# All 160 attention steps of the second branch moved into the segment loop of the first

## The chip, the cores and the metric

The kernel runs on one core of a Trainium2 chip. The metric is the device time of one execution in microseconds (us). A kernel is run several times in each round, beside the kernel before on the same chip, and the median of its runs is quoted. The profile page names the engines PE (matmul), PEld (its weight loads), DVE (VectorE), ACT (ScalarE), POOL (GpSimd) and SP (SyncE, which issues nearly all DMAs here).

## The reference, cut to what matters

Two attention branches over the same 2048 positions are mixed by a gate. Branch A goes through 64 segments of 32 rows one after the other, because the 8 memory rows of a segment come out of the one before it. Branch B attends causally inside four chunks of 512 rows, with 32 heads of 16 columns, and adds a linear-attention memory that the earlier chunks leave.

```python
# A: serial over 64 segments, 32 heads of 128
for s in range(n_seg):
    h = concatenate([mem, x[s*32:(s+1)*32]])        # 8 + 32 rows
    q, k, v = h @ Wq, h @ Wk, h @ Wv
    o = softmax(mask(q k^T * scale)) v
    o = o @ Wo
    mem = o[:8];  outs.append(o[8:])
# B: four chunks of 512 rows, 32 heads of 16
for s in range(4):
    a_dot = softmax(qs ks^T * scale + mask) vs
    a_mem = phi(qs) M / (phi(qs) z + 1e-6)
    o = g * a_mem + (1 - g) * a_dot
    M = M + phi(ks)^T vs;  z = z + sum(phi(ks))
# mix
out = gate * a + (1 - gate) * (b @ wo)
```

## The kernel before

The kernel is a Python program that emits instructions in a fixed order for each engine. Branch A's segment is a list of units (`A_ORDER`). Since A is a serial chain, work that does not depend on it is put between its units: the projections of the next segments' "left" rows (`Fc`, `Ff`), and the steps of B (`bS` scores, `bP` times V, `bT` the chain that divides and adds the memory term).

B's attention is cut into 16 jobs (four chunks, four groups of 8 heads) of ten steps each, 160 steps in all. A job first needs its keys and queries (`KTj`, `QTj`), then its values and memory (`Vj`, `pQj`, `MZj`), which the projections had stored in DRAM.

```python
def load(self, job, part):                       # class BAttn
    ...
    if part == "k":
        for e in range(2):
            for t in range(4):                   # eight DMAs of 16 KB
                o = 32 * t + 16 * e
                ld(v.KTj[par][e][o:o + 16, :], v.kTd[sb, f, o:o + 16, :], ...)
        ld(v.QTj[par][:, :], v.qTd[sb, f], ...)  # a ninth of 128 KB
        return
    ld(v.Vj[par][:, :, :], v.vd[sb, :, :, 136 * f:136 * (f + 1)], ...)
    if sb > 0:
        ld(v.pQj[par][:, :], ...);  ld(v.MZj[par][:, :], ...)

def scores(self):
    n = self.n; self.n += 1
    job, G, k = n // 10, (n // 5) % 2, n % 5     # G: which 4 of the 8 heads
    ...
    r = slice(64 * G + 32 * x, 64 * G + 32 * x + 32)    # partitions read
    ins = pe.matmul(..., KT[e][r, 128 * kc:128 * (kc + 1)], QT[r, q0:q0 + w], ...)
    ...
    if n % 10 == 9:                              # last step of the job:
        self.load_next(job, "k")                 # the next job's K and Q
```

`par` picks one of two buffers for the first 40 steps. These run ahead of the segment loop, between the pieces of the projections. For the other 120 steps, which run in segments 0 to 50, there is one buffer. The order of a segment, and the pace of the steps:

```python
n_pre = DEV.get("n_pre", 40)
for n in range(n_pre):                           # ahead of the segments
    bat.scores()
    while pieces and done < 10 + n * rate:
        piece()                                  # a projection
    ...
    if n > 1:
        bat.pv()
...
A_ORDER = """
    K1 K0 Q0 Q1 Fc TK0 TQ0 TK1 Ff bP TQ1 bT Fc S0 bS V0 M0 S1 N0 V1 M1 N1 PV0 Fc E0a E0b PV1 W0 E1a E1b W1 Fc bP bP bS
    WT bS Ff bT""".split()
...
nseg_b = DEV.get("nseg_b", 51)
target = min(bat.total, n_b0 + -(-(bat.total - n_b0) * (s + 1) // (nseg_b)))
def b_s():
    if bat.n < target and bat.n - bat.pv_n < 2:
        bat.scores()
```

`S`, `M`, `N`, `PV`, `E`, `W` and `WT` are A's own scores, sums, normalization, product with V, evacuation, output product and transposition into the next segment's memory rows. `N1` makes the tile `Pn_sb` that `PV1` reads.

## Time and profile before

The median is 1159.68 us; the profiled run's span is 1153.9 us. The first lines of the profile page of the kernel before: span, busy time of each engine, and three rows of the 40 slices (tenths of busy time, granted PE clock, DMA).

```profile
span 1153.9 us, 54295 instructions
...
PE 1012.0 (88%) x24359; PEld 559.7 (49%) x24389; DVE 491.1 (43%) x1229; ACT 692.1 (60%) x1427; POOL 248.7 (22%) x573
...
PE   4667769999999999999999999999999998988886
...
PEclk8798779999999999999999999999999998999999
DMA  9486310010101001010100001010100000000000
```

PE is at 4 to 7 tenths in the first six slices, and at 9 from there nearly to the end. So there are two stages. The table by stretches of the kernel before has the columns PE, PEld, DVE, ACT and POOL busy us with instruction counts, then granted clock, DMA share and GB/s. I cut it at the first pass of A (164 us), the first copy of memory rows into `hT` (188), the copy 56 segments later (1045) and the last copy (1132).

```profile
0.00:164.00 164.00, 104.20 (x871) 53.65 (x885) 54.57 (x106) 67.68 (x91) 85.46 (x176) 0.82 0.59 197
164.00:188.00 24.00, 22.25 (x462) 11.25 (x464) 8.34 (x18) 11.92 (x25) 1.60 (x5) 0.91 0.01 3
188.00:1045.00 857.00, 797.70 (x20687) 446.62 (x20696) 386.92 (x1006) 557.74 (x1181) 155.08 (x375) 1.00 0.06 17
1045.00:1132.00 87.00, 73.97 (x1993) 40.76 (x1992) 34.66 (x86) 46.38 (x112) 6.14 (x17) 1.00 0.04 9
1132.00:1154.00 22.00, 13.84 (x351) 7.42 (x352) 6.62 (x16) 8.39 (x20) 0.40 (x1) 0.94 0.03 8
```

In the first row PE is busy for 104.20 of 164 us, at a clock of 0.82: this is the stage that the change attacks. In the third row it is busy for 797.70 of 857 us at full clock: this stage is bound by PE.

Two places matter. The first is a job change, where the last step of one job is followed by the first step of the next, which needs new K and Q. In the timeline of the kernel before (start, duration, engine, line, operation, out<-in, count), the eight K loads are issued from 231.23 on, the Q load at 235.70, and the next score step comes at 238.79. Q had landed at 237.83, so nothing waited.

```profile
230.69 0.39 PE L726 MATMUL ps<-QTa,KTa 32*128 32x256 bf16 x4
231.23 4.43 SPq L685 DMA_DIRECT2D KTa<-scr_kTd  x8
...
235.70 0.42 SPq L685 DMA_DIRECT2D QTa<-scr_qTd  x1
```

The second is the gap between the two products with V (L1102), of which the second needs the normalized `Pn_sb`. Here a half left pass (L876, 0.62 us) stands between them, and 0.36 us of idle time are left.

```profile
516.32 0.27 PE L1102 MATMUL ps<-Pn_sb,V_sb 32*128 32x40 bf16 x16
...
516.64 0.62 PE L876 MATMUL ps<-Wv_sb,xL 128*32 128x512 bf16 x8
517.62 0.28 PE L1102 MATMUL ps<-Pn_sb,V_sb 32*128 32x40 bf16 x16 [0.36 <-DVE Pn_sb L1092]
517.92 2.18 PE L1139 MATMUL ps<-Wo_sb,OT_sb 128*32 128x512 bf16 x32
```

The view of waits of the kernel before sums them up (us in total, times, longest). Of the 13.1 us for Q, 11.8 are one wait ahead of the segments; in the middle of the segments they are 1.3.

```profile
PE ps L1102 <- DVE Pn_sb L1092: 25.4, 62, 0.9
...
PE ps L726 <- DMA QTa<-scr_qTd: 13.1, 5, 11.8
```

### The profile page before, as it was taken

What the parts mean: (1) busy time and instruction counts of PE and PEld (TensorE: products, weight loads), DVE (VectorE), ACT (ScalarE), POOL (GpSimd) and SP (SyncE); (2) the same over time, 40 slices, a digit from 0 to 9 for tenths busy, and PEclk for the clock granted to TensorE, in tenths of its full rate; (3) what the DMA queues carried; (4) which work ended last, traced back from release to release, by engine and by line L of the source; (5) the groups of instructions that cost most, each with busy time, mean ns of one, the idle gap of its engine ahead of it and who ended that gap; (6) DMA issues with size and microseconds to landing.
All of it is one profiled execution on the core that took longest, in us unless ns stands there. A gap on an engine that the chain in (4) does not pass through costs nothing. (4 is left out here: it accounts for less than half of the span.)

```text
span 1153.9 us, 54295 instructions
## 1 busy us (share of the span) xinstructions
PE 1012.0 (88%) x24359; PEld 559.7 (49%) x24389; DVE 491.1 (43%) x1229; ACT 692.1 (60%) x1427; POOL 248.7 (22%) x573
## 2 busy tenths in 40 slices
PE   4667769999999999999999999999999998988886
PEld 2333325555555555555555555555555554544443
DVE  2333334444444444444444444444444443434333
ACT  2455336666666666666666666666666664555554
POOL 6554431211212121212122111212122110000000
PEclk8798779999999999999999999999999998999999
DMA  9486310010101001010100001010100000000000
GB/s 309 141 278 226 105 62 3 3 32 4 36 5 27 13 11 29 8 32 8 27 12 23 12 9 31 8 33 7 28 12 23 18 3 21 3 12 4 12 12 7
DMA packets 50943, 47.59 MB, mean 41 GB/s; under 512 B 23184, under 2 KB 49176, under 8 KB 49176
## 3 DMA queue, kind: packets, MB, share of 16 engines
q1 hardware_dynamic: 50712, 44.13, 12.3%
q8 instruction: 192, 3.15, 1.1%
q14 instruction: 39, 0.32, 0.1%
HBM read 31.50 MB, written 12.61 MB: 38 GB/s over the span
## 5 line engine op out<-in xcount | busy, mean ns | idle before, releaser
L742 POOL TENSOR_SCALAR_AFFINE_SELECT PTa<-PTa 128x256 bf16<-128x256 bf16 (+1 forms) x205 | 90.1, 440 | 419.1 <-ACT PTa L734 387.6
L734 ACT ACTIVATE PTa<-ps 128x1024 bf16<-128x1024 f32 x147 | 150.4, 1024 | 42.2 <-PE ps L726 40.6
L876 PE MATMUL ps<-Wv_sb,hT 128*32 128x512 bf16 x2048 | 134.9, 381 | 2.0 <-ACT QT_sb L312 1.3
L312 ACT ACTIVATE QN_sb<-ps 128x512 bf16<-128x512 f32 x128 | 76.4, 597 | 89.5 <-PE ps L876 89.5
L876 PE MATMUL ps<-Wk_sb,hT 128*32 128x512 bf16 x2048 | 123.3, 383 | 3.7 <-DVE hT L1166 2.6
L1139 PE MATMUL ps<-Wo_sb,OT_sb 128*32 128x512 bf16 x2048 | 126.2, 381 | 0.1
L876 PE MATMUL ps<-Wq_sb,hT 128*32 128x512 bf16 x2048 | 121.6, 379 | 0.0
L314 DVE CAST V_sb<-ps 128x512 bf16<-128x512 f32 x128 | 88.5, 691 | 73.1 <-PE ps L1077 40.5
L1149 DVE TENSOR_TENSOR aW_sb<-ps,aW_sb 128x256 bf16<-128x256 f32 x128 | 48.4, 420 | 128.1 <-ACT aW_sb L312 126.1
L312 ACT ACTIVATE aW_sb<-ps 128x256 bf16<-128x256 f32 x128 | 42.2, 381 | 92.5 <-PE ps L1139 92.5
L1191 POOL COPY OTL<-OT_sb 128x256 bf16<-128x256 bf16 x64 | 25.4, 397 | 319.4 <-DVE OT_sb L314 319.4
L312 ACT ACTIVATE OT_sb<-ps 128x320 bf16<-128x320 f32 x192 | 75.7, 428 | 24.9 <-PE ps L1111 24.9
L312 ACT ACTIVATE QT_sb<-ps 128x512 bf16<-128x512 bf16 x128 | 77.0, 601 | 22.3 <-PE ps L885 22.3
L876 PEld LDWEIGHTS ps<-Wq_sb,hT 128*32 128x32 bf16 x2048 | 54.8, 97 | 55.8
L726 PE MATMUL ps<-QTa,KTa 32*128 32x512 bf16 (+1 forms) x448 | 55.6, 305 | 24.4 <-DMA QTa<-scr_qTd 13.1
L314 DVE CAST KN_sb<-ps 128x512 bf16<-128x512 f32 x64 | 44.2, 690 | 75.6 <-PE ps L876 75.6
L876 PEld LDWEIGHTS ps<-Wk_sb,hT 128*32 128x32 bf16 x2048 | 49.2, 97 | 53.5 <-DVE hT L1166 5.1
L314 DVE COPY KT_sb<-ps 128x512 bf16<-128x512 bf16 x64 | 27.2, 425 | 111.0 <-PE ps L885 111.0
L1139 PEld LDWEIGHTS ps<-Wo_sb,OT_sb 128*32 128x32 bf16 x2048 | 46.6, 95 | 49.9 <-ACT OT_sb L312 20.7
L876 PEld LDWEIGHTS ps<-Wv_sb,hT 128*32 128x32 bf16 x2048 | 47.2, 95 | 38.1 <-issue 6.7
L312 ACT ACTIVATE KN_sb<-ps 128x512 bf16<-128x512 f32 x64 | 38.2, 597 | 43.2 <-PE ps L876 43.0
L1081 ACT ACTIVATE R_sb<-ps 128x160 f32<-128x160 f32 x128 | 38.8, 303 | 33.7 <-PE ps L1077 33.3
(146 smaller groups left out, 1802.5 us busy)
## 6 DMA issues: line engine op xcount, KB each, us to landing
Wk_sb<-in_A_Wk_dram SPq DMA_DIRECT2D x4, 1024.0 KB, 7.9
Wq_sb<-in_A_Wq_dram SPq DMA_DIRECT2D x4, 1024.0 KB, 5.6
Wv_sb<-in_A_Wv_dram SPq DMA_DIRECT2D x4, 1024.0 KB, 6.4
Wo_sb<-in_A_Wo_dram SPq DMA_DIRECT2D x4, 1024.0 KB, 6.3
scr_vd<-V SPq DMA_DIRECT2D x16, 136.0 KB, 2.2
Wo_sb<-in_A_x_dram SPq DMA_DIRECT2D x4, 512.0 KB, 8.2
scr_kTd<-stgk SPq DMA_DIRECT2D x16, 128.0 KB, 3.9
scr_qTd<-stgq SPq DMA_DIRECT2D x16, 128.0 KB, 4.6
```

What stands on the lines that cost most here:

```text
L312: P.op("act", lambda a: a.activation(dst, src, ACT.Copy), reads=[v.rbank[k] for k in bks], writes=dres, name=name)
L314: P.op("dve", lambda d: d.tensor_copy(dst, src), reads=[v.rbank[k] for k in bks], writes=dres, name=name)
L726: ins = pe.matmul(v.pb[bks[x]][:, o:o + w], KT[e][r, 128 * kc:128 * (kc + 1)], QT[r, q0:q0 + w], start=True, stop=True, tile_position=(r.s ...
L734: P.op("act", lambda a: a.activation(pt[:, :, :], v.ps[:, bks[0]:bks[1] + 1, :], ACT.Exp, scale=v.SCALE_B), reads=[v.rbank[b] for b in bks ...
L742: P.op("gp", lambda g, mv=mv: g.affine_select(mv, mv, [[0, mv.shape[1]], [1, 128]], ALU.is_ge, 0.0, base=0, channel_multiplier=-1), reads= ...
L876: ins = pe.matmul(pb[bk][SEG * j:SEG * (j + 1), :], lhs(c), w_sb[:, c, n0:n0 + 512], start=(c == 0), stop=(c == C - 1))
L1081: P.op("act", lambda a: a.activation(R_sb[:, b, :], pb[bk][:, 224:384], ACT.Ln), reads=[rbank[bk]], writes=[Rs("R%d" % b)], name="ln%d_%d" ...
L1139: ins = pe.matmul(pb[bk][SEG * j:SEG * (j + 1), :], OT_sb[:, h, 0:SEG], Wo_sb[:, h, :], start=(b == 0 and i == 0), stop=(b == 1 and i == 3))
L1149: P.op("dve", lambda d, cs=cs: d.tensor_tensor(aW_sb[:, 1, cs], pb[bk][:, cs], aW_sb[:, 0, cs], ALU.subtract), reads=[rbank[bk], Rs("aWh%d ...
L1191: P.op("gp", lambda gq: gq.tensor_copy(OTL[par][:, :, 8 * r:8 * r + 8], OT_sb[:, :, SEG:L]), reads=[Rs("OT%d_%d" % (c, hf)) for c in range ...
```

## The change

The intent: B's first 40 steps stretch the stage before the segments, where PE is badly used. With all 160 steps in the segments, that stage holds projections alone. B then lags behind A, so A's finished rows are parked in DRAM until the B chunk of the same rows is through. The second set of job buffers goes, staging gets deeper, the pieces of the projections come in another order, part of their work moves from POOL to DVE, the engine assignment changes, and the left passes are no longer cut in halves. The diff, cut to its core:

```diff
-    n_pre = DEV.get("n_pre", 40)
-    bat = v.bat = BAttn(v, n_pre)
...
+    bat = v.bat = BAttn(v)
+    for n in range(len(pieces)):                      # projections only
...
+        pieces[n]()
...
     for part in "kv":
-        for job in range(2):
-            bat.load(job, part)
-    for n in range(n_pre):
-        bat.scores()
...
+        bat.load(0, part)
... (BAttn: one buffer throughout)
         if n % 10 == 9:
-            self.load_next(job, "k")
+            self.load(job + 1, "k")
... (pv: the chain of the job before is forced if its V load is not out yet)
+        while self.late and (job, "v") not in self.loaded:
+            self.run_late(1)
         self.load(job, "v")
...
 A_ORDER = """
-    K1 K0 Q0 Q1 Fc TK0 TQ0 TK1 Ff bP TQ1 bT Fc S0 bS V0 M0 S1 N0 V1 M1 N1 PV0 Fc E0a E0b PV1 W0 E1a E1b W1 Fc bP bP bS
-    WT bS Ff bT""".split()
+    bS K0 Q0 K1 Q1 TK0 TQ0 TK1 V0 bP TQ1 bP bT S0 Fc M0 S1 N0 V1 M1 PV0 E0a N1 E0b Ff PV1 W0 E1a E1b bS W1 Fc bS bP WT
+    Ff bT Ff""".split()
-A_ENG = dict(K0="dve", K1="act", Q0="act", Q1="act", V0="dve", V1="dve", TK0="dve", TK1="act",
-             TQ0="act", TQ1="act", E0a="act", E0b="act", E1a="act", E1b="dve", last=1)
+A_ENG = dict(K0="dve", K1="act", Q0="dve", Q1="act", V0="act", V1="dve", TK0="act", TK1="dve",
+             TQ0="dve", TQ1="act", E0a="act", E0b="act", E1a="dve", E1b="act", last=1)
...
-    n_b0, nseg_b = bat.n, DEV.get("nseg_b", 51)
+    n_b0, nseg_b = bat.n, DEV.get("nseg_b", 57)
... (left_units: one pass of four 128-row blocks instead of two halves)
-                for part in range(2):
-                    def u(...):
-                        proj(bk, lhs, w_sb, b, 2 * part, 2 * part + 2, ...)
+                def u(...):
+                    proj(bk, lhs, w_sb, b, ...)
... (A's rows parked, and fetched with B's rows for the last product)
+            P.dma(..., lambda sp: sp.dma_start(v.aTd[g], aT_st[par][:, :, :]), ...)
...
+        P.dma(..., lambda sp: sp.dma_start(aTg[:, :, :], v.aTd[g]), ...)
```

## The prediction

> What bounds it now. The page gives PE 88% of 1153.9 us, but there are two stages. Until 164.3 us (timeline: first pass with Wk and xL) the projections run with 40 of the 160 attention steps of B; the table by stretches shows PE 45 to 77% busy there, clock mostly 0.80 to 0.89, DMA 0.3 to 0.9. The 64 segments then take 990 us. With B steps in them PE is 93 to 94% busy at clock 1.00: about 15.2 us from one memory-row copy (hT, DVE) to the next, 0.9 of it PE idle, mostly 0.36 before the second PV (waits for Pn) and 0.32 before the WT transposition (timeline). So PE and its order bound the segments; evacuation chains and DMA bound the prologue.
>
> Removed. 40 steps leave the prologue. What stays is 60 projections of four 512-column matmuls (0.87 us at full clock in the timeline), transposes, and DMA: 16.5 us of first inputs, ten 1 MB weights at about 3.4, some 60 stores at 0.34, together 71 us; PE, from 7 us on, needs about as long. POOL leaves the phi chain (1.48 us each), staging is deeper. First pass at about 82 us (75 to 95): -82 us.
>
> Added, steady. A step costs PE 0.32 (scores) + 0.29 (PV) us; 2.8 instead of 2.35 steps in a segment, over 57 segments. Usually nothing stands between the two PVs now, so the chain from the second half's sums to Wo (1.8 us) shows about 1.0 us idle instead of 0.4; the WT wait shrinks, because the Fc there is a whole 0.87 us pass. About 15.5 us a segment: +19. Without the stall at 965-986 us: -6. Waits for Wo at the start: +3. A second row group is left for after the last segment; its DMAs (1.7 to 2.8 us each) are serial: +8. Fewer fillers in the last segments: +3.
>
> Added, new waits. KTj/QTj have one buffer. The next job's nine loads start when its predecessor's tenth score step is done, and land 6.4 to 7.2 us after the first issue (timeline). Before, the following step came a long stretch later: PE waited for QTa only 1.3 us in all segments. Now two score slots stand 2 us apart at the segment's end and a third opens the next one. By the order of instructions, 9 of 15 job changes fall there: 4 with about 6 us of waiting, 4 with 5, 1 with 3.6: 48 us. In four segments both PVs of a job change are neighbours, so the V load (3.6 us) is waited for: 14 us. The Trainium skill ("TensorE: Matmul & The Clock Gate", Part 1) says that an idle window of about 3.4 us halves the PE clock; the trace agrees once in the segments (3.8 us idle, 0.5 for 6.8 us). Estimate: +10.
>
> Sum of spans: 1154 - 82 + 19 - 6 + 3 + 8 + 3 + 62 + 10 = 1171. I lean a little lower for overlaps: 1168 us; 1130 to 1200 should hold it 8 times in 10. Faster by over 2%: 0.2; within: 0.48; slower: 0.32.
>
> Right if: first left pass near 82 us; PE waits for QTj on DMA of 35 to 55 us in 9 segments, for Vj of 10 to 15; clock dips after them; undisturbed B segments of about 15.5 us.
>
> Wrong if: stores behind weights hold the prologue longer, or the clock stays halved after most waits (slower); the new engine assignment closes the gap before the second PV (faster).

## The result, and the profile after

The changed kernel took 1195.99 us (median of 4 runs, 1193.82 to 1199.4) against 1159.55 (1157.56 to 1160.88) for the kernel before in the same rounds. The ratio is 1.0318, with a 95% interval of 1.0289 to 1.0347: slower by 3.2%. A ratio here and below is the mean time of one kernel's runs over that of the other's of the same rounds, so it is not quite the ratio of the quoted medians. The forecast of 1168 us had the right sign and was 28 us short; the time lies inside the range of 1130 to 1200. A slowdown by over 2% had been given a chance of 0.32, less than the 0.48 for no clear change.

The profile page of the changed kernel, the same rows:

```profile
span 1192.1 us, 54216 instructions
...
PE 1026.2 (86%) x24389; PEld 553.3 (46%) x24389; DVE 513.3 (43%) x1309; ACT 671.2 (56%) x1371; POOL 212.5 (18%) x544
...
PE   8968997899789799979998999698978899999874
...
PEclk9989999899989899999999999899989999999997
```

The first slices are now at 8 and 9, as intended. But the 9s of the long stage have holes, and at several of them the clock row has an 8. The table by stretches of the changed kernel, cut at the same events:

```profile
0.00:82.00 82.00, 66.08 (x425) 33.57 (x429) 46.19 (x94) 34.56 (x59) 24.65 (x91) 0.96 0.86 282
82.00:111.00 29.00, 24.58 (x480) 11.67 (x480) 8.98 (x20) 12.46 (x25) 1.96 (x6) 0.89 0.73 236
111.00:1068.00 957.00, 840.62 (x21119) 457.51 (x21118) 411.40 (x1077) 572.46 (x1162) 177.93 (x427) 0.97 0.08 20
1068.00:1158.00 90.00, 77.20 (x2012) 41.76 (x2012) 38.91 (x100) 43.17 (x106) 7.55 (x20) 0.98 0.06 16
1158.00:1192.00 34.00, 17.75 (x364) 8.82 (x361) 7.81 (x18) 8.54 (x20) 0.40 (x1) 0.78 0.11 28
```

The first stage gave 82 us back (164 to 82). The same 56 segments went from 857 to 957 us: PE is busy for 43 us more, and idle for 57 us more (116 instead of 59). Where the idle time sits is told by the waits of the changed kernel:

```profile
PE ps L704 <- DMA QTj<-scr_qTd: 40.5, 9, 5.1
...
PE ps L1078 <- DVE Pn_sb L1068: 39.1, 43, 1.1
...
PE ps L751 <- DMA MZj<-scr_mzd: 10.6, 3, 3.7
...
PE ps L751 <- DMA Vj<-scr_vd: 2.6, 1, 2.6
```

Nine of the 15 job changes wait for the K and Q loads (L704 is the score step), and three and one for the memory and value loads (L751 is the step's product with V). The timeline of the changed kernel at one of the nine shows how. The tenth step of a job is at 745.81, and the next score step stands only two units later:

```profile
745.81 0.39 PE L704 MATMUL ps<-QTj,KTj 32*128 32x256 bf16 x4
...
746.23 3.56 SPq L664 DMA_DIRECT2D KTj<-scr_kTd  x8
...
746.80 0.25 PE L1136 MATMUL ps<-selL,aW_sb 128*128 128x32 bf16 x4 [0.16 <-DVE aW_sb L1125]
...
749.84 0.42 SPq L664 DMA_DIRECT2D QTj<-scr_qTd  x1
...
752.01 0.61 PE L704 MATMUL ps<-QTj,KTj 32*128 32x512 bf16 x2 [4.96 <-DMA QTj<-scr_qTd]
752.55 1.90 PE L855 MATMUL ps<-Wk_sb,hT 128*32 128x512 bf16 x16
754.23 1.92 PE L855 MATMUL ps<-Wq_sb,hT 128*32 128x512 bf16 x16
755.94 1.78 PE L855 MATMUL ps<-Wk_sb,hT 128*32 128x512 bf16 x16
757.55 1.03 PE L855 MATMUL ps<-Wq_sb,hT 128*32 128x512 bf16 x16
```

Two things are to be read here. First, the nine loads are issued one after the other, about 0.45 us apart, and the last had landed at 751.88, 5.65 us after the first issue. Each of the nine lands within 1.5 to 2.0 us of its own issue. (At the other job changes in the segments of this kernel the loads are 0.45 to 0.60 us apart, and the last lands 5.6 to 7.2 us after the first issue.) The Trainium skill ("DMA: Bandwidth & Descriptors", section "Anatomy of one DMA — SWDGE (gpsimd) path") gives a fixed cost of about 2.0 us for a DMA of another path, most of it completion. The trace agrees in size for these loads from SP, and shows what that single figure does not: the issues of a list add up. Second, after the wait the passes of 16 matmuls start 1.7 us apart (752.55, 754.23, 755.94, 757.55), where a pass takes 0.87 us elsewhere: PE ran at half clock, from 750.6 to 757.4, for 6.8 us. The same skill ("TensorE: Matmul & The Clock Gate", Part 1, "What's actually happening") says that the clock halves after an idle window of about 3.4 us, and that the window runs free of the program. The trace agrees in kind and not in the length: each of the 13 waits for job loads in the segments, 2.65 to 5.12 us long, has one stretch of 3.4 or 6.8 us at 0.5 that begins before the wait ends or up to 0.6 us after it, and three of these waits are shorter than 3.4 us (2.65, 2.84 and 3.32). The 13 stretches are 65 us together; the kernel before has one of 6.8 us in its segments. The length of the wait alone doesn't decide: a wait of 2.63 us in e5 was followed by no such stretch. Part of a stretch is still waiting time: here PE waited until 752.01. Of the 65 us, 15 lie inside the waits, and in the other 50 PE is busy throughout.

A whole segment of this kind beside its undisturbed neighbours, in the table by stretches of the changed kernel:

```profile
731.00:747.00 16.00, 14.92 (x386) 8.24 (x384) 6.47 (x16) 10.94 (x22) 3.10 (x8) 1.00 0.01 4
747.00:775.00 28.00, 18.30 (x378) 9.01 (x376) 8.02 (x23) 9.88 (x21) 3.23 (x7) 0.82 0.11 27
```

With nearly the same number of matmuls it took 28 us instead of 16: 9.7 us idle instead of 1.1, and 3.4 us more of busy time for the same work, at a clock of 0.82.

The other new loss is small but comes in most segments. With the left passes whole and `Fc` moved away, nothing stands between the two products with V. In the timeline of the changed kernel the wait for `Pn_sb` is 0.94 us instead of 0.36:

```profile
120.43 0.27 PE L1078 MATMUL ps<-Pn_sb,V_sb 32*128 32x40 bf16 x16
120.55 0.25 PE L1087 MATMUL ps<-Pn_sb,VL 32*128 32x16 bf16 x16
121.73 0.28 PE L1078 MATMUL ps<-Pn_sb,V_sb 32*128 32x40 bf16 x16 [0.94 <-DVE Pn_sb L1068]
```

The span by parts, with a segment measured from one copy of memory rows (`hT` on DVE) to the next:

| part | before | after | difference |
|---|---|---|---|
| to the first pass of A | 164.3 | 81.9 | -82.4 |
| to the first memory-row copy | 23.6 | 28.7 | +5.1 |
| next 56 segments | 856.8 | 957.6 | +100.8 |
| six segments without B | 87.1 | 89.9 | +2.7 |
| to the end | 22.0 | 33.9 | +11.9 |
| span | 1153.9 | 1192.1 | +38.2 |

In the 56 segments of the changed kernel, 43 have a mean of 15.73 us, and 13 (the ones with a job change that waits) are together 76.8 us longer than that. So the +100.8 are 76.8 of disturbance and 24.0 in everything else.

### The profile page after: what moved, and what is told of

It reads as the page before. It is cut to its first block, busy times and chain, and to the rows that moved or that the text cites. A ratio compares the mean times of both kernels' runs of the same rounds, so it can differ in the third digit from the quotient of the medians. Undisturbed runs are those within 1.5% of the kernel's fastest.

```text
span 1192.1 us, 54216 instructions
## 1 busy us (share of the span) xinstructions
PE 1026.2 (86%) x24389; PEld 553.3 (46%) x24389; DVE 513.3 (43%) x1309; ACT 671.2 (56%) x1371; POOL 212.5 (18%) x544
## 4 chain that ended last, share of the span: by engine, by line
PE 73%; ACT 9%; DVE 7%; DMA 5%; SPq 3%; issue 3%; POOL 1%; ACTq 0%; POOLq 0%; DVEq 0%
PE ps L855 35%; PE ps L1115 8%; PE ps L864 6%; PE ps L704 4%; SPq L664 3%; PE ps L751 3%; PE ps L583 2%; ACT PT L712 2%; PE ps L558 2%; DVE Pn_sb L1064 2%; PE ps L1078 2%; DMA QTj<-scr_qTd 2%; PE ps L918 2%; PE ps L964 1%; ACT R_sb L1057 1%
## 5 line engine op out<-in xcount | busy, mean ns | idle before, releaser
L712 ACT ACTIVATE PT<-ps 128x1024 bf16<-128x1024 f32 x160 | 163.3, 1022 | 99.1 <-PE ps L704 95.3
L855 PE MATMUL ps<-Wk_sb,hT 128*32 128x512 bf16 x2048 | 142.5, 401 | 0.7 <-DVE hT L1142 0.6
L720 POOL TENSOR_SCALAR_AFFINE_SELECT PT<-PT 128x256 bf16<-128x256 bf16 (+1 forms) x224 | 98.4, 439 | 223.8 <-ACT PT L712 215.3
L855 PE MATMUL ps<-Wq_sb,hT 128*32 128x512 bf16 x2048 | 137.1, 389 | 0.0
L1169 POOL COPY OTL<-OT_sb 128x256 bf16<-128x256 bf16 x64 | 25.4, 397 | 545.3 <-DVE OT_sb L321 432.9
L319 ACT ACTIVATE KN_sb<-ps 128x512 bf16<-128x512 f32 x64 | 38.2, 597 | 128.7 <-PE ps L855 128.7
L704 PE MATMUL ps<-QTj,KTj 32*128 32x384 bf16 (+3 forms) x512 | 64.8, 310 | 41.5 <-DMA QTj<-scr_qTd 40.5
L1078 PE MATMUL ps<-Pn_sb,V_sb 32*128 32x40 bf16 x2048 | 36.4, 178 | 44.5 <-DVE Pn_sb L1068 39.1
L751 PEld LDWEIGHTS ps<-Vj,PT 128*128 128x128 bf16 x1280 | 44.5, 96 | 55.7 <-issue 39.4
L751 PE MATMUL ps<-Vj,PT 128*128 128x17 bf16 x1280 | 57.4, 172 | 14.9 <-DMA MZj<-scr_mzd 10.6
L321 DVE COPY QT_sb<-ps 128x512 bf16<-128x512 bf16 x64 | 27.2, 425 | 99.5 <-PE ps L864 99.5
L1064 DVE TENSOR_TENSOR Pn_sb<-P_sb,R_sb 128x160 bf16<-128x160 bf16 x128 | 44.1, 345 | 51.0 <-ACT R_sb L1060 42.2
```

The costliest lines, as they stand in the source:

```text
L319: P.op("act", lambda a: a.activation(dst, src, ACT.Copy), reads=[v.rbank[k] for k in bks], writes=dres, name=name)
L321: P.op("dve", lambda d: d.tensor_copy(dst, src), reads=[v.rbank[k] for k in bks], writes=dres, name=name)
L704: ins = pe.matmul(v.pb[bks[x]][:, o:o + w], KT[e][r, 128 * kc:128 * (kc + 1)], QT[r, q0:q0 + w], start=True, stop=True, tile_position=(r.s ...
L712: P.op("act", lambda a: a.activation(pt[:, :, :], v.ps[:, bks[0]:bks[1] + 1, :], ACT.Exp, scale=v.SCALE_B), reads=[v.rbank[b] for b in bks ...
L720: P.op("gp", lambda g, mv=mv: g.affine_select(mv, mv, [[0, mv.shape[1]], [1, 128]], ALU.is_ge, 0.0, base=0, channel_multiplier=-1), reads= ...
L751: ins = pe.matmul(v.pb[ob][:, o:o + 17], pt[:, x, col:col + 128], V[:, kc, 17 * h:17 * (h + 1)], start=first, stop=True, skip_group_check= ...
```

## Experiments

The theory: the gain of 82 us is real, and it is more than eaten by the single-buffered loads at the job changes, including the half clock after them. The rivals: the order and engine assignment of the segment are simply worse; or the 40 steps cost more in the segments than they freed. The kernel before had medians of 1159.78 (e1 to e4), 1160.65 (e5 to e8) and 1159.09 us (e9 and e10). Each edit is made to the changed kernel. All ten are faster than the changed kernel, the slowest (e4) by 28 us.

### e1_nseg56: another phase of the job changes

Nothing is changed but the pace, and with it where in the segment each job changes. By the order of instructions, 8 of the 15 changes then fall where there is time, and no chain is forced.

```diff
-    n_b0, nseg_b = bat.n, DEV.get("nseg_b", 57)
+    n_b0, nseg_b = bat.n, DEV.get("nseg_b", 56)
```

> One number changed: the 160 steps of B are spread over 56 segments instead of 57. Theory A (waits for single-buffered K/Q and V loads at job changes make the loss): counted from the order of the slots, 9 bad K changes (8 of them under 2 us apart) and 4 neighbouring V changes become 7 K changes of about 3.5 us and no V change. PE waits for QTj fall from 40.5 to about 25 us, for Vj/MZj from 15 to about 0, and the clock stays at 1.00 nearly throughout: 1140 to 1158 us. Theory B (the 40 moved steps simply cost more PE time in the segments than they cost ahead of them): same work, 1190 to 1200 us. Theory C (the new order with an empty gap between the two PVs makes the loss): 1190 to 1200 us.

Measured: 1151.47 us (1148.0 to 1155.78), ratio 0.9932 (0.9896 to 0.9967), correct. One constant is worth 44.5 us, and brings the kernel under the kernel before. The waits for QTj fell from 40.5 us in nine to 19.7 in six; those for Vj went. Six job changes still wait 3.1 to 3.6 us for QTj, and their segments are 5 to 6 us longer than the others, more than the wait: all six have a stretch at half clock of 3.4 or 6.8 us. (A seventh waits 2.1 us for DVE and has none.) One of the six, in the timeline of e1:

```profile
206.93 0.61 PE L704 MATMUL ps<-QTj,KTj 32*128 32x512 bf16 x2 [3.36 <-DMA QTj<-scr_qTd]
```

This speaks against both rivals: order, engines and number of steps are the same.

### e2_no_k_reload: K and Q loaded once

This takes the loads away, and with them the wait. The arithmetic is wrong, since all jobs use the K and Q of the first. The scores are so small here that the result still passed the comparison with the reference; it is not a version to keep.

```diff
         if part == "k":
+            if job:
+                return
             for e in range(2):
```

> Wrong results on purpose: K and Q of B are loaded for the first job only and never again, so no scores step can wait for a load. V is still reloaded. Theory A: waits for QTj 0 instead of 40.5 us, and with them most of the half-clock stretches; waits for V (15 us) stay: 1128 to 1145 us. Theories B and C: 1188 to 1198 us.

Measured: 1138.13 us (1133.87 to 1141.27), ratio 0.9824 (0.9795 to 0.9853). The K and Q loads cost 58 us of the 1195.99.

### e3_no_kv_reload: V and the memory kept as well

Wrong result (relative error 0.473). Jobs 0 and 4 still load, so that every buffer is filled.

```diff
+        if job not in (0, 4):
+            return
         ld(v.Vj[:, :, :], v.vd[sb, :, :, 136 * f:136 * (f + 1)], ...)
```

> Wrong results on purpose: neither K/Q nor V, pQ, MZ are reloaded after their first job. Theory A: the whole excess of the 13 disturbed segments, 77 us by the segment table of the trace, goes: 1112 to 1126 us, which is faster than the kernel before by 3 to 4%. Theories B and C: above 1185 us.

Measured: 1133.64 us (1131.62 to 1135.41), ratio 0.9776 (0.9749 to 0.9802). This was a miss: 4.5 us instead of the 12 or more that I expected over e2. The trace shows two reasons. Job 4's own load still waited (MZj, 3.4 us). And in the segments where both products of a job change are neighbours (`bP TQ1 bP`), the finishing chain of the old job is forced out in between, so the row transposition that closes the job comes one unit later than the chain that it depends on. In the timeline of e3, without any load, PE then waits for POOL's last addition:

```profile
723.64 0.59 PE L816 MATMUL ps<-ident,orow 128*128 128x128 bf16 x4 [2.54 <-POOL orow L807]
```

So not all of that loss belongs to the load; taking the load away uncovers the chain, and no run takes away the one without the other.

### e4_fill_pv: the gap between the products filled

`V0` moves between `S0` and `M0`, its eviction goes to DVE, and a left pass (`Fc`) stands before `PV1`. The job changes stay as bad as they are.

```diff
-    ... TK1 V0 bP TQ1 bP bT S0 Fc M0 S1 N0 V1 M1 PV0 E0a N1 E0b Ff PV1 ...
+    ... TK1 bP TQ1 bP bT S0 V0 M0 S1 N0 V1 M1 PV0 E0a N1 E0b Fc Ff PV1 ...
-    ... V0="act" ...
+    ... V0="dve" ...
```

> Order within a segment alone: the whole Fc pass moves from between S0 and M0 to between the two PVs, and V0 takes its old place between S0 and M0 (its eviction on DVE). The idle 0.94 us before the second PV should fall to about 0.2. Theory C: 0.6 to 0.9 us less in each of 60 segments, 1140 to 1160 us, waits for QTj unchanged at 35 to 45 us. If PE is bound by its work or the chain through Pn, OT and Wo merely moves its idle time: 1188 to 1200 us. Theory A: at most the 40 us of C, and the 77 us of the disturbed segments stay.

Measured: 1167.93 us (1165.35 to 1170.14), ratio 1.0071 (1.0044 to 1.0097), correct. The gain of 28 us is real, but smaller than the 36 us or more that were expected. In the waits of e4 the gap is closed, and the job changes are untouched. A new wait takes part of the gain back: PE waits 15.6 us, in 38 places, for V_sb on DVE, to which e4 moved one of its two evictions.

```profile
PE ps L704 <- DMA QTj<-scr_qTd: 39.8, 9, 5.1
PE ps L855 <- DVE V_sb L321: 15.6, 38, 0.8
...
PE ps L1078 <- DVE Pn_sb L1068: 3.7, 4, 0.9
```

### e5_k_by_halves: K and Q released in two halves

The remedy that needs no memory. (A second pair of K and Q buffers did not fit: the build failed at an allocation with 128 bytes of SBUF, the on-chip memory, left in each partition.) A job's steps 0 to 4 read partitions 0 to 63 of K and Q, its steps 5 to 9 read partitions 64 to 127. So the lower half is free after step 4, five steps before the change.

```diff
+    def load_k(self, job, G):
+        ...
+        for e in range(2):
+            for t in (2 * G, 2 * G + 1):
+                o = 32 * t + 16 * e
+                ld(v.KTj[e][o:o + 16, :], v.kTd[sb, f, o:o + 16, :], ...)
+        r = slice(64 * G, 64 * G + 64)
+        ld(v.QTj[r, :], v.qTd[sb, f, r, :], ...)
...
-        if n % 10 == 9:
-            self.load(job + 1, "k")
+        if k == 4:
+            self.load_k(job + 1, G)
```

> Correct results, pacing and order as in the change. K and Q of a job are used by heads in two halves of 64 partitions: steps 0 to 4 read the lower half, 5 to 9 the upper. Each half is released and reloaded on its own, so the next job's lower half loads while the upper is in use, in the same buffers. Theory A (K waits at job changes): waits for QTj fall from 40.5 to under 2 us without any wrong data, V changes stay: as without reload, 1130 to 1146 us. If the gain without reload came from the missing DMA traffic instead: 1180 to 1196 us.

Measured: 1137.81 us (1137.05 to 1141.66), ratio 0.9817 (0.9786 to 0.9848), correct. It gains as much as loading nothing at all (e2, 1138.13). All the bytes are loaded again here, so what e2 saved was the wait with what follows it, and not the traffic. No wait for QTj is left; those for MZj (10.6 us in 3) and Vj (2.6 in 1) are as before.

The Trainium skill ("DMA: Bandwidth & Descriptors", section "Rules for kernel authors") advises against two transfers to disjoint halves of the partitions, since they share the same engines. For bandwidth that may hold; no run here tests it. Here the halves pay, because a half can start when its own readers are done.

### e6_nseg56_fill: e1 and e4 together

> 56 segments for B and the Fc pass between the two PVs together. If the two losses are independent they add: 1151.5 - 28 = 1123 us, 1115 to 1133, faster than the kernel before by 3%. If filling the gap only helped by overlapping with the waits at job changes: 1140 to 1152 us.

Measured: 1128.22 us (1126.74 to 1131.05), ratio 0.9726 (0.97 to 0.9752), correct. Two edits that only move instructions, a constant and an order, are worth 68 us together; separately they gave 44.5 and 28. The losses are nearly independent.

### e7_kv_halves_fill: everything by halves, and the gap filled

e5, the same for V and the memory (68 of 136 columns each, released after the chain of their half), and e4's order.

```diff
+        part = "v%d" % G
+        while self.late and (job, part) not in self.loaded:
...
+        self.load(job + 1, "v%d" % G)                 # in the chain of half G
         if G == 1:
-            self.load(job + 1, "v")
+            self.load(job + 1, "p")
```

> 57 segments. K/Q and V/MZ by halves (pQ on its own), and Fc between the PVs. All 13 disturbed segments should become ordinary: 77 us of excess and about 30 us of the gap less than the change: 1080 to 1100 us, 5 to 7% faster than the kernel before. If V changes are bound by something else than the load (the run without V reload still showed 2.5 us waits for the row of a job, in segments where the chain was forced), they do not come back here either, because no chain is forced any more. If theory B holds (the moved steps cost more than they save ahead): not under 1150.

Measured: 1097.82 us (1096.46 to 1100.06), ratio 0.9463 (0.9438 to 0.9488), correct. This version beats both kernels: 5.4% faster than the kernel before. From the page and the table by stretches of e7:

```profile
span 1095.0 us, 54359 instructions
...
PE   7968999999999999999999998999999998999874
```

```profile
110.00:975.00 865.00, 815.82 (x21116) 452.39 (x21126) 442.86 (x1135) 544.45 (x1106) 178.40 (x427) 1.00 0.09 22
```

The holes are gone, and the 56 segments that took 957 us take 865 at full clock but for two stretches of 3.4 us. The loads that PE still waits for are the first x (4.5 us), Wo (1.3 us) and the two last row groups (7.8 us).

### e8_core_alone: the move with the old order, engines and half passes

This separates the rival "the new order is worse" from the move itself.

```diff
 A_ORDER = """
-    bS K0 Q0 K1 Q1 ... (the order of the changed kernel)
+    K1 K0 Q0 Q1 Fc TK0 TQ0 TK1 Ff bP TQ1 bT Fc S0 bS ... (the order of the kernel before)
... (A_ENG of the kernel before; left passes in halves again)
```

> The change without its new order, engine assignment and whole left passes: order, engines and half passes of the kernel before, all else (steps all in the loop over 57 segments, projections ahead, A rows parked) as in the change. With that order 4 of the 15 K changes fall on slots 0.7 us apart (about 6 us each), those to the next segment's slot do not wait, and 4 V changes are neighbours: waits for QTj about 24 us, V about 14, clock about 10; idle before the second PV 0.4 instead of 0.94. Sum: 1150 to 1172 us, 2 to 4% under the whole change. If the new order was a gain: above 1196.

Measured: 1159.51 us (1157.72 to 1163.69), ratio 0.9998 (0.9967 to 1.003), correct. So the new order, with its engines and whole passes, does cost 36.5 us. But the move with the old order gains nothing either, and its trace has the same trouble: PE waits 26.3 us for QTj in 10 job changes. The old order at 2.8 steps a segment is not safe; it was safe at the 2.35 of the kernel before.

### e9_kv_halves and e10_core_kv_halves: the halves alone, under both orders

e9 is the changed kernel with K, Q, V and memory by halves and nothing else; e10 is e8 with the same halves. If the losses of e8 and of the changed kernel are the loads, the two must come together.

> The change with K/Q and V/MZ loaded by halves and nothing else: its own order, 57 segments. Theory A puts 77 us on the 13 disturbed segments; K alone by halves took 58 of the run time, so V should take the other 17 to 21: 1117 to 1123 us, and then the gap between the PVs (run with both: 1098) is worth 19 to 25 us without waits, as against 28 with them. If V changes stay expensive for another reason: 1130 to 1138 us.

> The core alone (order, engines and half passes of the kernel before) with K/Q and V/MZ by halves. Its disturbed segments show 10 waits for QTj (26 us) and 3 for V (10 us), and half-clock stretches after them: 45 to 55 us of excess to go, 1104 to 1116 us. That would make the moved steps with the old order about 4% faster than the kernel before, and set the new order with its empty gap (the run with halves alone) behind the old one by about 10 us.

Measured: e9 1118.39 us (1115.7 to 1119.39), ratio 0.9638 (0.9609 to 0.9667); e10 1112.87 us (1108.75 to 1113.7), ratio 0.9588 (0.9561 to 0.9616); both correct. Of the 36.5 us between the two orders 5.5 are left. In e9 the 13 disturbed segments are 1.3 us longer than their neighbours together, instead of 76.8; the undisturbed ones have the same mean as in the changed kernel (15.74 and 15.73 us). The same 56 segments of e9, in its table by stretches, are at full clock:

```profile
110.00:993.00 883.00, 819.09 (x21141) 451.99 (x21138) 410.54 (x1079) 571.82 (x1162) 177.82 (x427) 1.00 0.09 22
```

For nearly the same number of matmuls PE is busy for 21.5 us less than in the changed kernel (840.62), and idle for 52.5 us less. The gap between the products is untouched in e9 (waits for Pn 42.2 us); with it filled, e7 is 20.6 us faster.

| kernel | us | against the changed kernel |
|---|---|---|
| changed | 1195.99 | |
| K and Q by halves (e5) | 1137.81 | -58.2 |
| V and memory too (e9) | 1118.39 | -77.6 |
| gap filled too (e7) | 1097.82 | -98.2 |
| gap alone filled (e4) | 1167.93 | -28.1 |

## Why the prediction was right and wrong

The mechanism was named correctly before the run: a gain of 82 us ahead of the segments, given back by waits at nine job changes and by the half clock after them. Two terms of the sum failed: the half clock, at +10 instead of about +23, and the steady segments, at +13 instead of +24. The forecast was low by 24 us between the sum of its terms as it was given (+14 with the lean) and the measured +38.2 of the spans. Term by term:

| term, as the prediction put it | forecast | measured |
|---|---|---|
| first pass at about 82 us | -82 | -82.4 |
| steady segments (+19), without the stall at 965-986 us (-6) | +13 | +24.0 |
| waits at job changes (48 + 14) | +62 | +53.7 |
| clock | +10 | about +23 |
| waits for Wo at the start | +3 | +5.1 (1.7 of it for Wo) |
| second row group at the end | +8 | +11.9 |
| fewer fillers | +3 | +2.7 |
| "I lean a little lower for overlaps" | -3 | 0 |

- **The prologue was right in its number.** The first left pass started at 81.9 us. By the prediction PE would work for about 71 us from 7 us on, so until about 78; its projections ended near 73, and then it waited 8.8 us, which no term has. A store that held a staging buffer kept DVE waiting for 5.0 us, and POOL, which copies the rows for the first pass, waited for DVE until 81. The prediction lists such stores only as a risk, so part of the agreement is luck.
- **The job changes were right in kind and place.** Nine waits for QTj of 40.5 us (forecast 35 to 55). The V part was put at 14 us for Vj; it was 13.2, three times for the memory tile MZj and once for Vj. The load that lands last is the one that is named. Together the waits came out 8 us under their term, and this hid part of what the clock and the steady term lacked: that is luck. e5 and e9 show that the two are worth 58 and 19 us with what follows them (in e9 the forced chain goes too).
- **The clock term failed most: "Estimate: +10" stands against about 23.** The disturbed segments were 76.8 us longer, and only 53.7 of that are waits. The prediction had cited the rule, had one stall in the trace before, which ran at half clock for 6.8 us, and named "the clock stays halved after most waits" as a way to be too low. It was so: all 13 waits had a stretch. If half of a stretch is lost, +10 stands for only three of 6.8 us. The traces bear the remainder of 23 us out in two ways. In the 13 stretches PE was busy for 50 us after the waits, and half of that is 25. And in e9, where waits and stretches are gone, PE needs 21.5 us less for the same segments. No run held the clock up with the waits in place.
- **The steady term failed next: "+19 ... -6" against +24.0.** Undisturbed segments took 15.73 us, not 15.5. The gap between the products was foreseen (1.0 us; 0.94 measured), and the recovery at the WT transposition that was credited against it came: over the whole run PE's waits there fell from 24.3 to 7.5 us, while those for `Pn_sb` rose from 25.4 to 39.1. What was low is PE's work. In e9, with no wait for a load and full clock, PE is busy for 819.09 us in the 56 segments, 21.4 more than before (797.70), and idle for only about 5 more. A plainer sum would have served: 40 more steps at the 0.61 us of PE time that the prediction itself gives are 24.4 us. e4 shows that filling the gap, with the moved `V0`, is worth 28 us, so idle time as large as the term could be avoided elsewhere.
- **Start and end were each a little low.** PE waited 1.7 us for Wo at the start; the rest of the +5.1 is not explained by a run. At the end two row groups each waited 4 us for their rows of B, one after the other; +8 was +11.9. The clock was halved there from 1177.3 us on, to the end, which the +8 had no term for; how much of the difference this makes was not separated.
- **The lean of -3 "for overlaps" had no number behind it**, and it went the wrong way.

The rival that the order was to blame falls in part: it costs 36.5 us as changed (e8), but 31 of these go when the loads are released by halves (e9 against e10). What costs is the distance between a job's last step and the next job's first, measured in the time that nine DMAs take. With that mended, moving the steps, with the edits of the first stage that came with it, is worth 46 us against the kernel before under the old order and engines (e10), and 63 with the new order filled (e7).

## What to carry to other kernels

When work moves into a loop that the compute engine bounds, ask of every single-buffered operand how long the new schedule leaves between its last reader and its next one, and compare that with the whole list of DMAs that refills it, not with one of them. If there is no room for a second buffer, look whether the readers use it in parts: releasing and refilling by halves needed no memory here and took 78 us away. And count stalls like the 13 here (2.65 to 5.12 us) at well over their length (together about 1.4 times), because PE came out of each of them at half clock.

## What the Trainium skill lacked or had wrong

- "DMA: Bandwidth & Descriptors" has a fixed cost for one DMA, but no measured time on trn2 for the interval at which SP issues a list of them (only a count of cycles for "previous generations", beside one for trn3). Here it was 0.45 us at the job change shown, for loads of 16 KB, so that nine loads had landed 5.65 us after the first issue (6.6 us at the one shown of the kernel before), while each took 1.5 to 2.0 us from its own issue.
- The same page, "Rules for kernel authors", says not to bother with transfers to disjoint halves of the partitions. It lacks the exception: where the halves come free at different times, loading them as two groups gained 58 us (e5), as much as no loads at all (e2).
- "TensorE: Matmul & The Clock Gate", section "HAM oscillation — how this bites in real kernels", counts half of the time at half clock as loss. Here the 13 stretches of 65 us would be 32 us by that rule, and about 23 us were lost on top of the 53.7 us of waits. Most stretches begin before the wait has ended, so part of them costs nothing more: 15 of the 65 us lie inside waits, and half of the other 50 is 25 us. The page doesn't separate this. The stretches were 3.4 or 6.8 us long, and a wait of 2.65 us sufficed to bring one.
